# Two attention decode blocks on one core: heads in quads instead of pairs, 64 KB rows per transfer

## The chip, the core and the metric

The kernel runs on one core of a Trainium2 chip. The core has five engines with queues of their own: TensorE (PE, matrix products into PSUM; its weight loads are shown as PEld), VectorE (DVE), ScalarE (ACT), GpSimd (POOL) and SyncE (SP, which here only issues DMAs). Sixteen DMA engines move data between HBM and SBUF, the on-chip memory of 128 partitions. A semaphore is a counter that one queue raises and another waits for. The metric is the device time of one execution in microseconds (us), lower is better; the figure for the kernel before is the median of three runs.

## What is computed

Two blocks, A and B, of the same shape and with inputs of their own, whose outputs are put side by side. For each block:

```python
# x [1,1,512]  k_cache, v_cache [1,32,8192,128]  wq [512,4096]  wo [4096,512]   all bf16
q = (x @ wq).reshape(B, Sq, H, Dh).transpose(0, 2, 1, 3)       # 32 heads of 128
scores = jnp.einsum("bhqd,bhkd->bhqk", q, k_cache) * (Dh ** -0.5)
p = softmax(scores, axis=-1)
o = jnp.einsum("bhqk,bhkd->bhqd", p, v_cache)
y = o.transpose(0, 2, 1, 3).reshape(B, Sq, H * Dh) @ wo        # [1,1,512]
```

One query per head meets 8192 keys and values. Each element of the caches is used once. K and V of one head are 2 MB each; both blocks together hold 128 MB of K and 128 MB of V, and 16 MB of weights (MB here as 2^20 bytes).

## The kernel before

**Tiling.** Two heads, a pair, are worked on at a time: 32 pairs (`NP`), 16 of each block. Head 0 of a pair lies on partitions 0 to 63, head 1 on 64 to 127, and a partition holds T = 128 consecutive keys of 128 elements, which are 32 KB in one piece in HBM. So one transfer of K or V of a pair is 128 rows of 32 KB, 4 MB (`load_k`, `load_v`). K has two slots in SBUF (`kn`), V has two (`vn`), and a further buffer `wbuf` of 32 KB per partition holds the weights: first wq of A, later wo of A, then wo of B. wq of B is read into V's slot 1 before V needs it.

**What happens to a pair n.** DVE multiplies K in place by the query, which stands in `qbc` on each partition, in four pieces of 32 keys (`plan_mul`, L313). PE sums over the 128 elements of a key in groups: 16 matmuls with the identity as weights, 512 columns each, add into one PSUM bank for half the keys (`plan_red`, L322), and DVE sums the last 8 columns of each key (`plan_sr`, L331). Then the maximum (`plan_max` L337, `plan_gmax` L343 and L346: a transposing matmul and a reduction), its spreading over the partitions and the exponentials on ACT (`plan_exp`, L356 to L367), the sum of the exponentials and its reciprocal (`plan_sum`, L372 and L375). For the output PE runs 128 matmuls per pair (`plan_pv`, L388), each with 128 columns of V as weights and the two heads' probabilities as a moving operand of two columns, and DVE scales (`plan_o`, L398).

**Order.** The loop over n writes each engine's instructions out by hand, one pair deep: in round n, K of pair n is multiplied and reduced while the output of pair n-1 is made. On PE a round is `plan_sum(n-1)`, both halves of `plan_red(n)`, the first half of `plan_pv(n-1)`, `plan_gmax(n)`, the second half of `plan_pv(n-1)`, and the spreading of `plan_exp(n)`. PE's instructions for rounds 1 to 30 stand in a hardware loop of two rounds each (`_emit_loop`), whose waits count with registers; a register is raised after the instruction that waited (L113). Since two rounds stand in the body, each instruction names its slot of K and V outright. The other engines' programs are not looped.

**DMAs.** All large loads are issued by SP, in this order: wq of A, K 0, wq of B, K 1, V 0, and from then on K n+1 and V n in turn. K n+1 waits until `plan_red(n-1)` is done with its slot (`red_done`), V n until `plan_pv(n-2)` is (`pv_done`). The last V is cut into two halves, and wo of B follows in five parts that shrink (16, 8, 4, 2 and 2 heads; `WOG`), so that the output projection (`plan_wo`, L440) can follow them.

Of the kernel before, what the change touches and what calls it, by code (L numbers as in the profile page):

```python
# [74 lines left out]
def _emit_loop(e, rounds):  # L75
# [30 lines left out]
    with e.Fori(0, len(rounds)):  # L106
        for k, (waits, it) in enumerate(body):
            for i, (ctr, v, d) in enumerate(waits):
                e.wait_ge(ctr.sem, regs.get((k, i), v))
            _emit(e, [it])  # L110
            for i, (ctr, v, d) in enumerate(waits):
                if d:
                    e.reg_add(regs[k, i], regs[k, i], d)  # L113


def bass_concat_heads__mha_block_cached__gqa_block_cached__decode_kernel(
# [26 lines left out]
    HP = P // 2  # L143
    T = Sk // HP
    assert T == 128
    PA = H // 2
    NP = NA * PA
    NK = NV = 2
    CT = 32
    NCH = T // CT  # L150
    HT = T // 2
    DW = 512 // HT
# [3 lines left out]
    RG = [32, 16, 8, 4, 2]  # L156

    with ExitStack() as st:
# [7 lines left out]
        vn = sb("vn", [P, NV, T, Dh], BF16)  # L166
        wbuf = sb("wbuf", [P, C * H * Dh], BF16)
        wq_buf = [wbuf[:], vn[:, 1].rearrange("p t d -> p (t d)")]
        wq_sb = [b.rearrange("p (c n) -> p c n", c=C) for b in wq_buf]
        wo_sb = wbuf[:].rearrange("p (j n) -> p j n", n=NOUT)  # L170
        qbc = sb("qbc", [P, NP, Dh], BF16)
        pt = sb("pt", [P, 2, T, 2], BF16)
        s_sb = sb("s_sb", [P, 2, T], F32)
        xrow = sb("xrow", [1, NA, D], BF16)
        xb = sb("xb", [P, NA, C, P], BF16)
# [4 lines left out]
        hrow = sb("hrow", [1, 2, P], F32)  # L180
        m1 = sb("m1", [P, 2], F32)
        gm = sb("gm", [1, 2, 2], F32)
        negb = sb("negb", [P, NP], F32)
        rsum = sb("rsum", [P, 2, 2], F32)
        rinv = sb("rinv", [P, NP, 2], F32)
# [13 lines left out]
        acc = ps("acc", [P, 2, 512])  # L199
# [13 lines left out]
        s_wo = [ctr("s_wo%d" % i) for i in range(5)]  # L213
        s_v2 = ctr("s_v2")
        s_k = [ctr("s_k%d" % i) for i in range(NK)]
        s_v = [ctr("s_v%d" % i) for i in range(NV)]
# [20 lines left out]
        const(lambda e: e.memset(hrow[0:1, 0, 0:HP], 1.0), [i_h0])  # L237
        const(lambda e: e.memset(hrow[0:1, 1, HP:P], 1.0))
# [7 lines left out]

        def load_k(n):
            a, i = divmod(n, PA)
            src = ks[a][0, 2 * i:2 * i + 2].rearrange("h (p t) d -> (h p) (t d)", p=HP)
            k_in[n] = dma("SP", kn[:, n % NK].rearrange("p t d -> p (t d)"), src, s_k[n % NK],  # L250
                          [red_done.get(n - NK)])

        def load_v(n, parts=1):
            a, i = divmod(n, PA)
            src = vs[a][0, 2 * i:2 * i + 2].rearrange("h (p t) d -> (h p) (t d)", p=HP)
            dst = vn[:, n % NV].rearrange("p t d -> p (t d)")
            w = T * Dh // parts
            v_in[n] = [dma("SP", dst[:, i * w:(i + 1) * w], src[:, i * w:(i + 1) * w],
                           s_v2 if i else s_v[n % NV],
                           [q_done[1] if n == 1 else pv_done.get(n - NV)])  # L260
                       for i in range(parts)]
# [4 lines left out]
        def load_wo(a, g):  # L266
            h0, n = WOG[a][g]
            src = wos[a][h0 * Dh:(h0 + n) * Dh, :].rearrange("(p j) n -> p (j n)", p=P)
            wo_in[a, g] = dma("SP", wo_sb[:, h0:h0 + n, :].rearrange("p j n -> p (j n)"), src, s_wo[g],
                              [q_done[0] if a == 0 else wo_done[0]])  # L270
# [16 lines left out]
        def plan_q(a, j):  # L287

            def mm(e):
                r = None  # L290
                for hh in range(2):
                    for c in range(C):
                        w = wq_sb[a][:, c, 8 * j * Dh:8 * (j + 1) * Dh].rearrange(
                            "p (i h d) -> p i h d", h=2, d=Dh)[:, :, hh, :]
# [7 lines left out]
            n0 = a * PA + 4 * j  # L302
# [6 lines left out]
        mul_done, sr_done, p_done, m_done, r_done, o_done = {}, {}, {}, {}, {}, {}  # L309

# [6 lines left out]
        def plan_red(n, h):  # L317

            def mm(e):
                r = None  # L320
                for i in range(Dh // DW):
                    r = e.matmul(  # L322
                        rps[:, h, :].rearrange("p (t d) -> p t d", d=DW), ident[:],
                        kn[:, n % NK, h * HT:(h + 1) * HT, i * DW:(i + 1) * DW],
                        start=(i == 0), stop=(i == Dh // DW - 1))
                return r
            last = (h + 1) * HT // CT - 1
            red_done[n] = op("PE", mm, c_red, [i_ident, mul_done[n, last], sr_done.get((n - 1, h))])

        def plan_sr(n, h):  # L330
            sr_done[n, h] = op("DVE", lambda e: e.tensor_reduce(  # L331
                s_sb[:, n % 2, h * HT:(h + 1) * HT],
                rps[:, h, :].rearrange("p (t d) -> p t d", d=DW), AX.X, ALU.add),
                c_sr, [red_done[n], p_done.get(n - 2)])

        def plan_max(n):
            m_done[n] = op("DVE", lambda e: e.tensor_reduce(  # L337
                m1[:, n % 2:n % 2 + 1], s_sb[:, n % 2, :], AX.X, ALU.max), c_dve, [sr_done[n, 1]])
# [3 lines left out]
        def plan_gmax(n):  # L342
            m = op("PE", lambda e: e.matmul(mtp[0:1, 0:P], m1[:, n % 2:n % 2 + 1], ident_f[:],  # L343
# [3 lines left out]
                gm[:, n % 2, :], mtp[0:1, 0:P].rearrange("o (h p) -> o h p", h=2), AX.X, ALU.max),  # L347
                c_dve, [m])
# [3 lines left out]
        def plan_exp(n):  # L352
            def bc(e):
                r = None
                for h in range(2):
                    r = e.matmul(bmp[:, 0:1], hrow[0:1, h, :], gm[0:1, n % 2, h:h + 1],  # L356
                                 start=(h == 0), stop=(h == 1))
# [5 lines left out]
            wait("ACT", pv_done.get(n - 2))  # L363
            wait("ACT", i_pool)
            for h in range(2):
                q = slice(h * HP, (h + 1) * HP)
                p_done[n] = op("ACT", lambda e, h=h, q=q: e.activation(  # L367
                    pt[q, n % 2, :, h], s_sb[q, n % 2, :], AF.Exp, bias=negb[q, n:n + 1],
                    scale=scale, accum_out=rsum[q, n % 2, h:h + 1]), c_act)

        def plan_sum(n):
            m = op("PE", lambda e: e.matmul(misc[:, 0:2], ones_f[:], rsum[:, n % 2, :],  # L372
# [3 lines left out]
                rinv[:, n, :], misc[:, 0:2]), c_dve, [m])  # L376

        def plan_pv(n, t0, t1):
            parts = v_in[n]
            for i in range(t0 * len(parts) // T, (t1 * len(parts) - 1) // T + 1):  # L380
                wait("PE", parts[i])
            wait("PE", p_done[n])
            wait("PE", o_done.get(n - 2))

            def mm(e):
                r = None
                for t in range(t0, t1):
                    r = e.matmul(acc[:, n % 2, 0:2], vn[:, n % NV, t, :], pt[:, n % 2, t, :],  # L388
# [7 lines left out]
        def plan_o(n):  # L396
            a, i = divmod(n, PA)
            o_done[n] = op("DVE", lambda e: e.tensor_tensor(  # L398
                oD[:, a, 2 * i:2 * i + 2], acc[:, n % 2, 0:2], rinv[:, n, :], ALU.mult),
# [17 lines left out]
        def plan_relayout(a, g):  # L417
# [8 lines left out]
                c_dve, [sel_ready[n], o_done[a * PA + (h0 + n) // 2 - 1], z_free.get(z)])  # L426
# [5 lines left out]
        def plan_wo(a, g):  # L432
# [3 lines left out]
            def mm(e):  # L436
                r = None
                for j in range(h0, h0 + n):
                    for i in range(NQ):
                        r = e.matmul(qyp[:, i:i + 1], wo_sb[:, j, i * P:(i + 1) * P],  # L440
# [9 lines left out]
        def plan_out():  # L450
            m = op("PE", lambda e: e.matmul(bmp[0:NA * NQ, 0:P], yT[:].rearrange("p a q -> p (a q)"),  # L451
                                            ident[:], start=True, stop=True),
                   c_pe, [qy_free[0], nb_done[NP - 1]])
# [5 lines left out]
        L0, L1 = 1, 31  # L459
        marks = {}  # L460

        load_wq(0)
        load_k(0)
        load_wq(1)
        plan_sel()
        for j in range(4):
            plan_q(0, j)
        for n in range(NP + 1):
            marks[n] = len(pl.prog["PE"])
            last = n == NP  # L470
            if n == L1:
                plan_relayout(0, 0)
                for g in range(3):
                    plan_relayout(1, g)
                plan_wo(0, 0)
            if n + 1 < NP:
                load_k(n + 1)
            if n == 1:
                for j in range(4):
                    plan_q(1, j)  # L480
                marks[n] = len(pl.prog["PE"])
            if not last:
                load_v(n, 2 if n == NP - 1 else 1)
            if n == 12:
                load_wo(0, 0)
            if n == NP - 1:
                for g in range(len(WOG[1])):
                    load_wo(1, g)
            if not last:
                plan_mul(n, 0)  # L490
                plan_mul(n, 1)
            if n == L1:
                plan_y(0)
            if n > 0:
                plan_sum(n - 1)
            if not last:
                plan_red(n, 0)
                plan_mul(n, 2)
                plan_mul(n, 3)
                plan_sr(n, 0)  # L500
                plan_red(n, 1)
            if n > 0:
                plan_pv(n - 1, 0, HT)
            if not last:
                plan_sr(n, 1)
                plan_max(n)
                plan_gmax(n)
            if n > 0:
                plan_pv(n - 1, HT, T)
            if not last:  # L510
                plan_exp(n)
            if n > 0:
                plan_o(n - 1)
            if n >= L1:
                plan_relayout(1, n - L1 + 3)
        for g in range(len(WOG[1])):
# [4 lines left out]
        for name, at in (("SP", block.sync), ("PE", block.tensor), ("ACT", block.scalar),  # L521
                         ("DVE", block.vector), ("POOL", block.gpsimd)):
            @at
            def _(e, name=name):
                prog = pl.prog[name]
                if name != "PE":
                    _emit(e, prog)
                    return
                _emit(e, prog[:marks[L0]])
                _emit_loop(e, [prog[marks[n]:marks[n + 2]] for n in range(L0, L1, 2)])  # L530
# [29 lines left out]
```

## Time and profile before

| | |
|---|---|
| median of three runs (671.5 to 672.41) | 671.81 us |
| the profiled execution | 671.82 us, of which its span is 670.0 us |
| HBM read over the span | 285.21 MB (10^6 bytes), mean 426 GB/s |
| mean granted clock of TensorE | 0.742 |
| DVE's multiply of K, L313 | 128 times, 2283 ns each |
| DVE's waits for K of block B, L313 | 15, together 29.4 us |

The span runs from the first to the last instruction. Engines' busy times overlap each other; a busy share says only how full an engine is, not whether the end waits for it. The DMA rows of the page give the share of time in which the 16 DMA engines had a packet in hand. A packet is one row of a transfer: 32 KB for most here, less for parts of wo, and 4 bytes for the semaphore write with which each of the 16 engines ends its part of a transfer. The granted clock tells at what share of its full speed TensorE was allowed to run.

### The profile page before, as it was taken

The numbers are of one execution on the slowest core, as the hardware profiler recorded it, in microseconds if no ns is written. First come the engines' busy times: TensorE is split into PE (matmuls) and PEld (weight loads), VectorE is DVE, ScalarE is ACT, GpSimd is POOL, SyncE is SP. The second block draws the span as 40 slices with busy tenths as digits, with TensorE's granted clock in tenths as the row PEclk, the third lists the DMA queues.
The fourth block names the chain that finished last, engine by engine and source line by source line (L and its number), as shares of the span: only waits on it lengthen the run. The fifth ranks groups of instructions, "written<-read, shape, count | busy, mean of one in ns | idle before, by whom it ended". The sixth has DMA issues, their size and how long they took to land.

```text
span 670.0 us, 12431 instructions
## 1 busy us (share of the span) xinstructions
PE 473.1 (71%) x5711; PEld 276.2 (41%) x5711; DVE 359.6 (54%) x345; ACT 43.9 (7%) x171; POOL 2.1 (0%) x13
## 2 busy tenths in 40 slices
PE   2677876766777776664667776676687766768887
PEld 1224443434444343441344443344454334444456
DVE  1545456665555666515655556665555656555561
ACT  1120000000000000000000000000000000000000
POOL 1000000000000000000000000000000000000000
PEclk9977876667787666786677876667878766788766
DMA  9999999999999999999999999999999999999996
GB/s 376 438 433 422 427 436 435 432 428 425 439 434 434 426 425 436 438 430 430 423 436 438 430 430 425 436 436 432 430 425 436 436 431 428 428 434 434 433 416 272
DMA packets 10545, 285.39 MB, mean 426 GB/s; under 512 B 1186, under 2 KB 1188, under 8 KB 1572
## 3 DMA queue, kind: packets, MB, share of 16 engines
q1 hardware_dynamic: 10528, 285.22, 99.1%
q8 instruction: 8, 0.13, 0.1%
q14 instruction: 5, 0.04, 0.0%
q10 hardware_dynamic: 4, 0.00, 0.0%
HBM read 285.21 MB, written 0.00 MB: 426 GB/s over the span
## 4 chain that ended last, share of the span: by engine, by line
DMA 65%; PE 23%; DVE 7%; issue 4%; SPq 0%
DMA kn<-in_A_k_cache_dram 31%; DMA kn<-in_B_k_cache_dram 30%; PE rps L322 22%; DVE kn L313 7%; DMA wbuf<-in_B_wo_dram 3%; PE qyp L440 1%; PE acc L388 0%; SPq L222 0%; PE bmp L356 0%; PE misc L427 0%; DVE zb L423 0%; DVE o L429 0%; PE mtp L343 0%; PE bmp L451 0%; DVE out_q L454 0%
## 5 line engine op out<-in xcount | busy, mean ns | idle before, releaser
L322 PE MATMUL rps<-kn,ident 128*128 128x512 bf16 x1024 | 294.6, 459 | 134.6 <-DVE kn L313 134.6
L313 DVE TENSOR_TENSOR kn<-kn,qbc 128x4096 bf16<-128x4096 bf16 x128 | 286.8, 2283 | 88.4 <-DMA kn<-in_A_k_cache_dram 59.0
L322 PEld LDWEIGHTS rps<-kn,ident 128*128 128x128 bf16 x1024 | 114.6, 115 | 302.5 <-DVE kn L313 132.6
L388 PEld LDWEIGHTS acc<-pt,vn 128*128 128x128 bf16 x4096 | 110.5, 97 | 14.3 <-issue 6.9
L331 DVE TENSOR_REDUCE s_sb<-rps 128x64 f32<-128x512 f32 x64 | 44.3, 692 | 132.2 <-PE rps L322 132.2
L388 PE MATMUL acc<-pt,vn 128*128 128x2 bf16 x4096 | 112.8, 163 | 0.0
L372 PE MATMUL misc<-rsum,ones_f 128*128 128x2 f32 x64 | 18.2, 355 | 39.5 <-ACT pt L367 38.8
L360 ACT ACTIVATE negb<-bmp 128x1 f32<-128x1 f32 x32 | 5.5, 171 | 587.8 <-PE bmp L356 587.8
L372 PEld LDWEIGHTS misc<-rsum,ones_f 128*128 128x128 f32 x64 | 15.5, 301 | 42.9 <-ACT pt L367 41.3
L398 DVE TENSOR_TENSOR oD<-acc,rinv 128x2 bf16<-128x2 f32 x32 | 5.1, 160 | 47.6 <-PE acc L388 47.6
L367 ACT ACTIVATE pt<-s_sb,negb 64x128 bf16<-64x128 f32 x64 | 27.8, 435 | 1.9
L346 DVE TENSOR_REDUCE gm<-mtp 1x2 f32<-1x128 f32 x32 | 8.9, 279 | 27.8 <-PE mtp L343 27.8
L356 PE MATMUL bmp<-gm,hrow 1*128 1x1 f32 x128 | 23.2, 282 | 0.5 <-DVE gm L346 0.5
L356 PEld LDWEIGHTS bmp<-gm,hrow 1*128 1x128 f32 x128 | 20.6, 226 | 1.3 <-issue 0.7
L343 PE MATMUL mtp<-ident_f,m 128*1 128x128 f32 x64 | 12.1, 271 | 1.1 <-DVE m L337 1.1
L295 PE MATMUL qyp<-wbuf,xb 128*64 128x512 bf16 x32 | 7.7, 632 | 6.2 <-DMA wbuf<-in_A_wq_dram 4.1
L367 ACT ACTIVATION_READ_ACCUMULATOR pt<-s_sb,negb 64x1 f32 x64 | 11.6, 182 | 0.0
L337 DVE TENSOR_REDUCE m<-s_sb 128x1 f32<-128x128 f32 x32 | 9.2, 286 | 1.1
L295 PE MATMUL qyp<-vn,xb 128*64 128x512 bf16 x32 | 6.6, 554 | 2.3 <-ACT qbc L303 2.3
L440 PE MATMUL qyp<-o,wbuf 128*128 128x1 bf16 x256 | 7.6, 165 | 0.5 <-DMA wbuf<-in_B_wo_dram 0.3
L440 PEld LDWEIGHTS qyp<-o,wbuf 128*128 128x128 bf16 x256 | 7.2, 104 | 0.7 <-issue 0.4
L375 DVE RECIPROCAL rinv<-misc 128x2 f32<-128x2 f32 x32 | 5.3, 164 | 3.4 <-PE misc L372 3.4
(34 smaller groups left out, 27.4 us busy)
## 6 DMA issues: line engine op xcount, KB each, us to landing
kn<-in_A_k_cache_dram SPq DMA_DIRECT2D x16, 4096.0 KB, 25.3
vn<-in_A_v_cache_dram SPq DMA_DIRECT2D x16, 4096.0 KB, 31.4
kn<-in_B_k_cache_dram SPq DMA_DIRECT2D x16, 4096.0 KB, 25.4
vn<-in_B_v_cache_dram SPq DMA_DIRECT2D x15, 4096.0 KB, 31.5
wbuf<-in_A_wq_dram SPq DMA_DIRECT2D x1, 4096.0 KB, 12.4
vn<-in_B_wq_dram SPq DMA_DIRECT2D x1, 4096.0 KB, 30.8
wbuf<-in_A_wo_dram SPq DMA_DIRECT2D x1, 4096.0 KB, 41.2
vn<-in_B_v_cache_dram SPq DMA_DIRECT2D x2, 2048.0 KB, 18.5
```

The lines of the kernel that those rows point to most:

```text
L295: r = e.matmul(qyp[hh * HP:(hh + 1) * HP, :].rearrange("p (i d) -> p i d", d=Dh), xb[:, a, c, hh * HP:(hh + 1) * HP], w, start=(c == 0), s ...
L313: mul_done[n, c] = op("DVE", lambda e: e.tensor_tensor(k, k, qbc[:, n:n + 1, :].broadcast_to([P, CT, Dh]), ALU.mult), c_mul, [k_in[n], qbc ...
L322: r = e.matmul(rps[:, h, :].rearrange("p (t d) -> p t d", d=DW), ident[:], kn[:, n % NK, h * HT:(h + 1) * HT, i * DW:(i + 1) * DW], start= ...
L331: sr_done[n, h] = op("DVE", lambda e: e.tensor_reduce(s_sb[:, n % 2, h * HT:(h + 1) * HT], rps[:, h, :].rearrange("p (t d) -> p t d", d=DW ...
L337: m_done[n] = op("DVE", lambda e: e.tensor_reduce(m1[:, n % 2:n % 2 + 1], s_sb[:, n % 2, :], AX.X, ALU.max), c_dve, [sr_done[n, 1]])
L343: m = op("PE", lambda e: e.matmul(mtp[0:1, 0:P], m1[:, n % 2:n % 2 + 1], ident_f[:], start=True, stop=True), c_pe, [m_done[n], i_identf, g ...
L346: gm_done[n] = op("DVE", lambda e: e.tensor_reduce(gm[:, n % 2, :], mtp[0:1, 0:P].rearrange("o (h p) -> o h p", h=2), AX.X, ALU.max), c_dv ...
L356: r = e.matmul(bmp[:, 0:1], hrow[0:1, h, :], gm[0:1, n % 2, h:h + 1], start=(h == 0), stop=(h == 1))
L367: p_done[n] = op("ACT", lambda e, h=h, q=q: e.activation(pt[q, n % 2, :, h], s_sb[q, n % 2, :], AF.Exp, bias=negb[q, n:n + 1], scale=scale ...
L372: m = op("PE", lambda e: e.matmul(misc[:, 0:2], ones_f[:], rsum[:, n % 2, :], start=True, stop=True), c_pe, [p_done[n], misc_free[0]])
L388: r = e.matmul(acc[:, n % 2, 0:2], vn[:, n % NV, t, :], pt[:, n % 2, t, :], start=(t == 0), stop=(t == T - 1))
L440: r = e.matmul(qyp[:, i:i + 1], wo_sb[:, j, i * P:(i + 1) * P], o2[:, a, j:j + 1], start=(j == 0 and i == 0), stop=(j == H - 1 and i == NQ ...
```

## The change

Four heads, a quad, are worked on at a time: 16 rounds (`NM`) in place of 32. A head now lies on 32 partitions, and each partition holds T = 256 keys, 64 KB in one piece. One transfer of K or V is 128 rows of 64 KB, 8 MB. K has two slots of this size, V has one, and `wbuf` is gone: both blocks' wq are read into V's slot, both blocks' wo into the K slot of quad 14 after it has been reduced, and x and its spread copy `xb` lie in K's slot 1 at the start.

```diff
-    HP = P // 2
+    G = 4
+    HP = P // G
     T = Sk // HP
-    NK = NV = 2
-    CT = 32
+    NK = 2
+    CT = 64
+    VLAST = (0, T // 2, T // 2 + CT, T)
...
-        vn = sb("vn", [P, NV, T, Dh], BF16)
-        wbuf = sb("wbuf", [P, C * H * Dh], BF16)
-        wq_buf = [wbuf[:], vn[:, 1].rearrange("p t d -> p (t d)")]
+        vn = sb("vn", [P, T, Dh], BF16)
+        wq_buf = [flat(vn[:])[:, a * W:(a + 1) * W] for a in range(NA)]
+        KX, KW = 1, (NM - 2) % NK
+        wo_sb = [flat(kn[:, KW])[:, a * W:(a + 1) * W].rearrange("p (j n) -> p j n", n=NOUT)
+                 for a in range(NA)]
+        xb = flat(kn[:, KX])[:, 0:NA * C * P].rearrange("p (a c m) -> p a c m", a=NA, c=C)
...
         def load_k(n):
+            k_in[n] = dma("SP", flat(kn[:, n % NK]), quad(ks, n), s_k[n % NK],
+                          [q_done[1] if n == KX else red_done.get(n - NK)])
+        def load_v(n, cuts=(0, T)):
+            dst, src = flat(vn[:]), quad(vs, n)
+            v_in[n] = [(t0, dma("SP", dst[:, t0 * Dh:t1 * Dh], src[:, t0 * Dh:t1 * Dh], s_v[i],
+                                [q_done[1] if n == 0 else pv_done[n - 1]]))
+                       for i, (t0, t1) in enumerate(zip(cuts, cuts[1:]))]
         def load_wo(a, g):
...
+                              s_wo[a][g], [red_done[NM - 2]])
```

The probabilities, the scores, their sums and the output's PSUM bank (`pt`, `s_sb`, `rsum`, `acc`) have one buffer where they had two. DVE multiplies in four pieces of 64 keys, and PE and DVE reduce each piece by itself (16 matmuls and one `plan_sr` for each), where a pair had two. PE's loop has one round in its body, 15 times; K's slot comes from the loop's counter, so the matmuls of `plan_red` take their address from a register.

```diff
-    with e.Fori(0, len(rounds)):
+    with e.Fori(0, len(rounds)) as r:
+        enter(r)
...
+                    if slot[0] is None:
+                        k = kn[:, n % NK, t, d]
+                    else:
+                        k = kn[:, bass.ds(slot[0], 1), t, d].rearrange("p o t d -> p (o t) d")
...
+                def enter(r):
+                    slot[0] = (r + L0) % NK
```

The order of a round and of the ends is written anew:

```diff
+        load_wq(0)
+        load_wq(1)
+        load_k(0)
...
+        for n in range(NM):
+            if n + 1 < NM:
+                load_k(n + 1)
+            else:
+                load_wo(0, 0)
+                load_wo(1, 0)
+            plan_mul(n, 0)
+            if n > 0:
+                plan_sum(n - 1)
+            plan_red(n, 0)
+            plan_mul(n, 1)
+            plan_red(n, 1)
+            plan_sr(n, 0)
+            plan_mul(n, 2)
+            plan_red(n, 2)
+            plan_sr(n, 1)
+            plan_mul(n, 3)
+            plan_sr(n, 2)
+            if n > 0:
+                plan_pv(n - 1, 0, T)
+                plan_o(n - 1)
+            plan_red(n, 3)
+            plan_sr(n, 3)
+            plan_max(n)
+            plan_gmax(n)
+            plan_exp(n)
+            load_v(n, VLAST if n == NM - 1 else (0, T))
+        for g in range(1, len(WOG[1])):
+            load_wo(1, g)
+        plan_relayout(0, 0)
...
+        plan_wo(1, 0)
+        plan_sum(NM - 1)
+        for t0, t1 in zip(VLAST, VLAST[1:]):
+            plan_pv(NM - 1, t0, t1)
+        plan_o(NM - 1)
+        for g in range(1, 3):
+            plan_wo(1, g)
+        for g in range(3, len(WOG[1])):
+            plan_relayout(1, g)
+        for g in range(3, len(WOG[1])):
+            plan_wo(1, g)
```

So `plan_pv(n-1)`, 256 matmuls in one run, stands on PE ahead of the last quarter of `plan_red(n)`, and DVE's `plan_o(n-1)`, which waits for it, ahead of the last `plan_sr(n)`. V n is issued when `plan_pv(n-1)` is done, K n+2 when `plan_red(n)` is. The last V comes in three parts (4, 2 and 2 MB), behind wo of A and the first half of wo of B, and the four smaller parts of wo of B come last.

In PE's program as built, each of the 64 `plan_red` matmuls of a loop round has one instruction of fused register operations ahead of it (three operations; five for the first of a round) that works out its address. The loop's body has 730 PE instructions, weight loads counted, for one round of four heads; before it had 673 for two rounds of two heads.

## Prediction

> **What bounds the kernel now.** I read the slices of the span first, then the DMA queues, the chain that ended last, and one round of the timeline.
>
> ```profile
> DMA  9999999999999999999999999999999999999996
> DMA packets 10545, 285.39 MB, mean 426 GB/s; under 512 B 1186, under 2 KB 1188, under 8 KB 1572
> q1 hardware_dynamic: 10528, 285.22, 99.1%
> DMA 65%; PE 23%; DVE 7%; issue 4%; SPq 0%
> ```
>
> The DMA engines have a packet in hand in every slice, 99.1% of the span on the one queue. The chain names PE and DVE too, but only where it follows the release of K's slot; the queue never ran dry there. The packet records (start, duration, bytes of each) confirm it: the bulk runs from 1.85 to 666.6 us, and its packets add up to 663.5 us per engine, so all idling together is some 1.3 us. After the last packet come 3.4 us: its notice, 8 matmuls, the copy, the store. The kernel is a DMA stream with 1.85 us ahead of it and 3.4 behind.
>
> One round before (a pair), from the timeline:
>
> ```profile
> 403.51 4.49 DVE L313 TENSOR_TENSOR kn<-kn,qbc 128x4096 bf16<-128x4096 bf16 x2 [2.20 <-DMA kn<-in_B_k_cache_dram]
> 408.06 9.41 PE L322 MATMUL rps<-kn,ident 128*128 128x512 bf16 x32 [4.53 <-DVE kn L313]
> 417.31 1.75 PE L388 MATMUL acc<-pt,vn 128*128 128x2 bf16 x64
> 417.50 0.33 SPq L222 DMA_DIRECT2D kn<-in_B_k_cache_dram  x1
> 421.08 0.33 SPq L222 DMA_DIRECT2D vn<-in_B_v_cache_dram  x1
> 422.94 4.49 DVE L313 TENSOR_TENSOR kn<-kn,qbc 128x4096 bf16<-128x4096 bf16 x2 [1.68 <-DMA kn<-in_B_k_cache_dram]
> ```
>
> DVE starts a pair when K lands, every 19.5 us, and waits for it; K and V are released 15 us and 11 us before the queue reaches them. Compute is covered by DMA.
>
> **What the change saves in the stream.** The bytes stay the same; the packets get larger. Median packet durations by size: 2 KB 84 ns, 4 KB 159, 8 KB 311, 16 KB 614, 32 KB 1218. Twice the half minus the whole is 9, 7, 8 and 10 ns: a fixed price of some 9 ns per packet. No packet of 64 KB is in the trace; extended by the same step it takes 2 x 1218 - 9 = 2427 ns. The bounds for this unknown: the split keeps 32 KB pieces (saving nothing), or the fixed price is 10 ns. I take 9. Sixty-two full transfers (7936 rows of 32 KB) become 31 (3968 of 64 KB); the last V has 128 rows of 32 KB and 256 of 16 KB in both. So 3968 x 9 ns / 16 engines = 2.2 us. SP's loads fall from 73 to 42, each ends with 16 semaphore packets of 9 ns: 31 x 9 ns = 0.3 us. Together -2.5 us, between 0 and -2.8.
>
> The Trainium skill, "DMA: Bandwidth & Descriptors", section "Latency and other measured facts", speaks against wider rows: row pitches at large powers of two slow HBM copies, 214 GB/s falling to 207 at 512 KiB and 164 at 2 MiB. Here the 32 KB pitch shows nothing of it (1st and 99th percentile of the 32 KB packets 1213 and 1225 ns) and the new pitch is 64 KB, far below. By the rule's first step (3.3%) an estimate would be some 20 us more; by the row, nothing. I go by the row.
>
> **Whether compute stays covered.** A quad's K and V pass in 16 packets per engine, 16 x 2.427 = 38.8 us; V n-1 lands half a period after K n. With S the landing of K n, from these rows:
>
> ```profile
> 408.10:412.70 4.60, 4.60 (x11) 1.59 (x12) 0.50 0.94 406
> 413.00:417.00 4.00, 4.00 (x20) 1.85 (x19) 1.00 1.05 451
> L388 PE MATMUL acc<-pt,vn 128*128 128x2 bf16 x4096 | 112.8, 163 | 0.0
> L331 DVE TENSOR_REDUCE s_sb<-rps 128x64 f32<-128x512 f32 x64 | 44.3, 692 | 132.2 <-PE rps L322 132.2
> ```
>
> (The first two are L322's stretches of one round: matmuls in brackets, then the granted clock.) A red matmul takes 0.42 us at clock 0.50 and 0.21 at 1.00; the clock rises some 5 us after PE begins. One multiply of 64 keys is two of 2283 ns, 4.5 us.
>
> - DVE mul 0 to S+4.5. PE red 0, cold: 11 at 0.42, 5 at 0.21, to S+10.4. Red 1 to S+13.8. DVE sr 0 waits for red 0, so mul 2 ends at S+15.6; red 2 to S+19.1; mul 3 at S+20.8.
> - V n-1 has landed at S+19.4. PV is 256 matmuls; 64 took 1.75 us (also at clock 0.50 in the tail: 128 in 3.55), so 7.0 us to S+26.4. That releases V n.
> - Red 3, assumed cold again after PV, 6 us to S+32.4: K n+2 is released. Sr 0.7, maximum 0.4, transposing matmul and reduction 1.2: DVE is free at S+34.8.
>
> K n+1 lands at S+38.8, so a round has 4 us to spare. V n is released at S+26.4 and the queue reaches it at S+38.8: 12 us. K n+2, S+32.4 against S+58: 26 us. The single V slot costs nothing because K n+1 fills the queue meanwhile; without that cover the queue would idle the 7 us of PV each round, 112 us in all. ACT's four exponentials (0.435 us for 128 columns, at most twice that for 256, plus 0.18 each) take up to 4.2 us after DVE's end, before the next multiply has ended. SP's waits are in the order of release (V n, then K n+2), so neither holds up the other.
>
> **Register addresses.** Each red matmul has a fused register operation ahead. Rows: 37 ns for a fused one, 32 for a single (L113). If it ran beside the array: 0; in series: 64 x 37 ns = 2.4 us per round, inside the 4 to spare. How PE issues a matmul whose address is in a register is not in the trace; bounds are 0.21 us (hidden) and the nearest instruction whose addresses a queue works out, SP's DMA issue, 0.33 + 0.04 = 0.37 us. I take hidden, as the register rows are nearest. At 0.37 red 1 and 2 grow by 5.1 us: 39.9 against 38.8, 1.1 x 15 rounds plus some 7 at the start: +23.
>
> **Start.** Wq of both land at about 12.5 and 22.8 us (in the trace K 0, second 4 MB in line, was there at 22.86). Two groups of 16 matmuls for block B (8 took 1.93 us, plus 0.75 until the next) end near 31; K 1 and V 0 are issued then, while K 0 transfers until 1.85 + 2 x 9.75 + 19.4 = 40.8. DVE's first multiply moves from 22.9 to 41.2 with no gap in the stream. Round 0 without PV ends at 41.2 + 26.7 = 67.9, later than K 1 landed; PV 0 ends at 67.9 + 26.2 = 94.1 and releases V 1, which the queue reaches at 99.0. This is the thinnest place: 5 us, of which about 1 goes from issue to first packet.
>
> **End.** Wo of A and half of B (14.6 us of packets) lie between V 14 and the last V, whose wait for PV 14 (S+26.4) ends before S+34. After its last part 5.1 us of wo follow. PV's 64 matmuls, the scaling, 32 and 16 matmuls of L440 fit beside these; two relayouts of 0.65 us remain, so the last matmuls come some 0.2 us later than before. Its 3.4 us become 3.6.
>
> **Sum.** 671.82 - 2.2 - 0.3 + 0.2 = 669.5 us; the profiled execution lies 0.01 us over the median. Own range 668.8 to 670.4.
>
> **Rivals.**
> - Slower: PE's rounds outgrow the transfers. If a red matmul took 0.42 us throughout (the clock held at 0.50, or the register path that slow), the chain is 4.5 + 64 x 0.42 + 7.0 + 2.9 = 41.3 us, 2.5 over; with V 1's gap of 9 and V 15's of 7, 14 x 2.5 + 16 = 51: 720 us. It decides from about 0.38 us per matmul. For: PV drops the clock, and red 3 comes after it. Against: in each round before, the clock rose within 6 us of red's start. With the milder 0.37 it gives 692. Chance 0.15 for both.
>
> The skill's "TensorE: Matmul & The Clock Gate", Part 1, says full clock comes after some 3.4 us of sustained activity and is lost after an idle window. The trace's 4.8 us is later; by the page's figure red 0 would end 1.4 us sooner, which the wait for K hides.
>
> - No change: rows are cut to 32 KB pieces, or 64 KB packets have no lower price: 671.82 - 0.3 + 0.2 = 671.7. For: no such packet is shown. Against: the price has been fixed over four doublings. Chance 0.13.
> - Start gap alone: reds in round 0 and 1 at 0.42 rather than my mix delay V 1 by up to 9 us past its margin: 670 to 679, middle 674. Against: nothing loads PE's clock there differently. Chance 0.09.
> - Packets of 64 KB a little slower per byte: 1% of 622 us is 6.2, so 676. For: no such row. Against: 32 KB rows spread over 1% only, 1213 to 1225 ns. Chance 0.04.
>
> **Numbers.** Forecast 0.59. Range 668.5 to 679: it holds all but the first rival, 0.85, less 0.03 at the edges. Faster than 670.5 (0.2%, about what a measurement here can tell from none): 0.59 less the upper edge plus little, 0.58. Within: 0.16, from no change and the edges. Slower: 0.26.
>
> **What would show it.** Right: 64 KB packets of about 2427 ns, the DMA row full in all slices, DVE waiting some 4 us per round for K, SP waiting only for PE with the queue still filled. Wrong: holes in the DMA row (at 95 us: start; in each round: PE), red matmuls over 0.38 us on average, packets of 32 KB, or packets over 2450 ns.

## The result, and the profile after

| | before | after |
|---|---|---|
| median, 5 runs each | 671.81 us (671.5 to 672.41) | 719.92 us (719.38 to 720.44) |
| ratio, 95% interval | | 1.0716 (1.0701 to 1.073) |
| profiled execution: span | 670.0 us | 718.7 us |
| first to last large packet | 1.85 to 666.6 us | 1.84 to 711.9 us |
| large packets' time per engine | 663.5 us | 670.1 us |
| stretches in which under 8 of the 16 DMA engines were busy (over 0.3 us each) | none | 15, together 38.5 us |
| after the last packet | 3.4 us | 6.8 us |

The last four rows are summed from the packet records. The span grew by 48.7 us: 38.5 of holes in the stream, 6.6 of packet time, 3.4 of tail; the rest is at the packets' edges. The 6.6 are a net figure: the larger packets save 2.7 us, and in 14 of the 15 holes the first packet of each engine behind the hole takes some 3.1 us instead of 2.42. The page of the changed kernel shows the same: the slices, the queue and the chain that ended last.

```profile
PEclk9558786676667577677668677667757667766865
DMA  9999948999999998999999898989899898989785
q1 hardware_dynamic: 6064, 285.22, 93.3%
PE 69%; DVE 16%; ACT 8%; DMA 6%; issue 2%; SPq 0%
```

The DMA row, all nines but the last digit before, has a dent in the sixth slice, then an 8 now and then, and in the second half in nearly every other slice. The chain was 65% DMA before; now it is PE, DVE and ACT, and DMA only until the first K has landed. The kernel is no longer a stream of transfers but a chain of computation. One stretch of the stages table (busy us and count of PE, PEld, DVE, ACT, POOL, then clock, DMA share, GB/s) shows the dent, the hole near 100 us:

```profile
99.50:112.00 12.50, 12.50 (x275) 8.77 (x274) 5.79 (x4) 0.00 (x0) 0.00 (x0) 0.77 0.08 25
```

And one round, from the timeline, with lines left out (start, duration, what; in brackets the idle time ahead of it and what ended it). Below, mul, red and sr with a number stand for `plan_mul`, `plan_red` and `plan_sr` of that piece of a quad:

```profile
308.88 6.65 PE L401 MATMUL acc<-pt,vn 128*128 128x4 bf16 x256
315.39 6.45 PE L334 MATMUL rps<-kn,ident 128*128 x16
315.56 0.33 SPq L230 DMA_DIRECT2D vn<-in_A_v_cache_dram  x1
321.88 0.33 SPq L230 DMA_DIRECT2D kn<-in_B_k_cache_dram  x1
323.71 4.40 DVE L320 TENSOR_TENSOR kn<-kn,qbc 128x8192 bf16<-128x8192 bf16 x1
328.86 0.59 PE L385 MATMUL misc<-rsum,ones_f 128*128 128x4 f32 x2 [3.82 <-ACT pt L380]
329.31 9.78 PE L334 MATMUL rps<-kn,ident 128*128 x32
329.49 0.18 DVE L388 RECIPROCAL rinv<-misc 128x4 f32<-128x4 f32 x1 [1.38 <-PE misc L385]
329.59 4.39 DVE L320 TENSOR_TENSOR kn<-kn,qbc 128x8192 bf16<-128x8192 bf16 x1
339.13 0.69 DVE L343 TENSOR_REDUCE s_sb<-rps 128x64 f32<-128x512 f32 x1 [5.14 <-PE rps L334]
339.74 4.42 DVE L320 TENSOR_TENSOR kn<-kn,qbc 128x8192 bf16<-128x8192 bf16 x1
344.29 5.67 PE L334 MATMUL rps<-kn,ident 128*128 x16 [5.20 <-DVE kn L320]
```

Red 0 and red 1 run as one block of 32 matmuls from 329.3 to 339.1. DVE's reduction of piece 0 (L343) starts when the whole block is over, not after its first 16. Multiply 2 stands behind that reduction on DVE, so red 2 cannot start before 344.3, and PE idles 5.2 us. In that time the granted clock falls to half (at 341.65) and red 2 takes 5.67 us, where the same 16 matmuls take 3.6 at full clock. From one red 0 to the next is 41.0 us in the later rounds; the transfers need 38.8.

The reason lies in two lines of the changed kernel. Every piece writes the same entry of the dictionary, and the round records red 1 ahead of the reduction of piece 0:

```python
red_done[n] = op("PE", mm, c_red, [...])          # plan_red(n, c), for every c
... c_sr, [red_done[n], p_done.get(n - 1)])       # plan_sr(n, c): the newest red recorded, not its own
```

`plan_sr(n, 0)` therefore waits for red 1 and `plan_sr(n, 1)` for red 2. The kernel before recorded `plan_sr(n, 0)` ahead of the second `plan_red`, so the same entry was the right one there. In a round with PV, sr 1's wait lies beside PV, on which red 3 has to wait anyway; round 0 has no PV, and there red 2 and red 3 both start late and at half clock. Its maximum comes at 78.0 us, against 66.3 us in the first run below, in which this wait alone is mended; that delay, passed on to V 1, is the hole near 100 us. The waits of DVE add up to (total us, times, longest):

```profile
DVE s_sb L343 <- PE rps L334: 272.5, 48, 6.2
DVE rinv L388 <- PE misc L385: 23.1, 16, 2.5
```

### The profile page after: what moved, and what is told of

It reads as the page before. It is cut to its first block, busy times and chain, and to the rows that moved or that the text cites. A ratio compares the mean times of both kernels' runs of the same rounds, so it can differ in the third digit from the quotient of the medians.

```text
span 718.7 us, 12990 instructions
## 1 busy us (share of the span) xinstructions
PE 500.1 (70%) x5647; PEld 269.8 (38%) x5647; DVE 341.7 (48%) x217; ACT 62.5 (9%) x151; POOL 2.8 (0%) x15
## 4 chain that ended last, share of the span: by engine, by line
PE 69%; DVE 16%; ACT 8%; DMA 6%; issue 2%; SPq 0%
PE rps L334 48%; PE acc L401 15%; DVE kn L320 11%; ACT pt L380 7%; DMA kn<-in_A_k_cache_dram 6%; DVE s_sb L343 3%; PE bmp L368 3%; PE misc L385 1%; PE qyp L453 1%; DVE m L349 1%; PE mtp L355 1%; DVE gm L358 1%; ACT negb L372 0%; PE misc L440 0%; DVE zb L436 0%
## 5 line engine op out<-in xcount | busy, mean ns | idle before, releaser
L334 PE MATMUL rps<-kn,ident 128*128 (+1 forms) x1024 | 348.4, 519 | 107.6 <-DVE kn L320 107.6
L320 DVE TENSOR_TENSOR kn<-kn,qbc 128x8192 bf16<-128x8192 bf16 x64 | 282.0, 4408 | 38.2 <-DMA kn<-in_A_k_cache_dram 38.2
L334 PEld LDWEIGHTS rps<-kn,ident 128*128 128x128 bf16 x1024 | 128.5, 128 | 314.8 <-issue 262.3
L343 DVE TENSOR_REDUCE s_sb<-rps 128x64 f32<-128x512 f32 x64 | 44.2, 690 | 272.5 <-PE rps L334 272.5
L401 PE MATMUL acc<-pt,vn 128*128 128x4 bf16 x4096 | 107.0, 165 | 4.2 <-issue 4.2
L380 ACT ACTIVATE pt<-s_sb,negb 32x256 bf16<-32x256 f32 x64 | 54.9, 858 | 2.1 <-ACT negb L372 0.2
L385 PE MATMUL misc<-rsum,ones_f 128*128 128x4 f32 x32 | 9.4, 364 | 57.5 <-ACT pt L380 57.5
L385 PEld LDWEIGHTS misc<-rsum,ones_f 128*128 128x128 f32 x32 | 8.0, 311 | 58.8 <-ACT pt L380 58.8
L380 ACT ACTIVATION_READ_ACCUMULATOR pt<-s_sb,negb 32x1 f32 x64 | 15.9, 248 | 0.0
L301 PE MATMUL qyp<-vn,kn 128*32 128x512 bf16 x64 | 7.7, 623 | 10.9 <-DMA vn<-in_B_wq_dram 5.1
L453 PE MATMUL qyp<-o,kn 128*128 128x1 bf16 x256 | 7.7, 165 | 0.8 <-issue 0.5
L301 PEld LDWEIGHTS qyp<-vn,kn 128*32 128x32 bf16 x64 | 2.3, 128 | 15.6 <-issue 6.4
```

The source lines that it names most:

```text
L301: r = e.matmul(qyp[hh * HP:(hh + 1) * HP, :].rearrange("p (i d) -> p i d", d=Dh), xb[:, a, c, hh * HP:(hh + 1) * HP], w, start=(c == 0), s ...
L320: mul_done[n, c] = op("DVE", lambda e: e.tensor_tensor(k, k, qbc[:, n:n + 1, :].broadcast_to([P, CT, Dh]), ALU.mult), c_mul, [k_in[n], qbc ...
L334: r = e.matmul(rps[:, c % 2, :].rearrange("p (t d) -> p t d", d=DW), ident[:], k, start=(i == 0), stop=(i == Dh // DW - 1))
L343: sr_done[n, c] = op("DVE", lambda e: e.tensor_reduce(s_sb[:, c * CT:(c + 1) * CT], rps[:, c % 2, :].rearrange("p (t d) -> p t d", d=DW), ...
L380: p_done[n] = op("ACT", lambda e, h=h, q=q: e.activation(pt[q, :, h], s_sb[q, :], AF.Exp, bias=negb[q, n:n + 1], scale=scale, accum_out=rs ...
L385: m = op("PE", lambda e: e.matmul(misc[:, 0:G], ones_f[:], rsum[:], start=True, stop=True), c_pe, [p_done[n], misc_free[0]])
```

## The experiments

The ratios are to runs of the kernel before, made beside each kernel on the same chip. A round is called covered when DVE waits in it for K's transfer.

**Own waits.** Each reduction waits for its own piece.

```diff
-            red_done[n] = op("PE", mm, c_red, [
+            red_done[n] = red_part[n, c] = op("PE", mm, c_red, [
...
-                c_sr, [red_done[n], p_done.get(n - 1)])
+                c_sr, [red_part[n, c], p_done.get(n - 1)])
```

> Each DVE reduction (plan_sr) of a piece waits for its own piece's matmuls instead of the newest planned ones; nothing else changes. Theory (the shared wait): sr 0 starts some 3.5 us sooner in a round, mul 2 and red 2 with it, red 2 falls from 5.7 to about 3.4 us because PE no longer idles 5 us ahead of it; the round falls from 40.95 us to the 38.8 of the transfers, the 1.5 us hole of each round and the 12.7 us hole near 100 us close: 668 to 674 us. Rival (register addresses slow the matmuls): under 1% change, 713 to 720. Rival (PE at half clock after PV is what costs): only the wait shrinks, 700 to 710.

Measured: 671.33 us (12 runs, 670.36 to 673.32), ratio 0.9999 (0.9987 to 1.001). A round from its timeline, with lines left out (the first line is the block of red 0 and red 1, cut by the window of the view):

```profile
379.51 9.29 PE L335 MATMUL rps<-kn,ident 128*128 x31
385.38 0.69 DVE L344 TENSOR_REDUCE s_sb<-rps 128x64 f32<-128x512 f32 x1 [2.07 <-PE rps L335]
385.99 4.42 DVE L321 TENSOR_TENSOR kn<-kn,qbc 128x8192 bf16<-128x8192 bf16 x1
390.55 3.62 PE L335 MATMUL rps<-kn,ident 128*128 x16 [1.75 <-DVE kn L321]
394.01 6.74 PE L402 MATMUL acc<-pt,vn 128*128 128x4 bf16 x256
400.60 5.73 PE L335 MATMUL rps<-kn,ident 128*128 x16
413.19 4.42 DVE L321 TENSOR_TENSOR kn<-kn,qbc 128x8192 bf16<-128x8192 bf16 x1 [4.92 <-DMA kn<-in_B_k_cache_dram]
```

The reduction now starts in the middle of the block, red 2 follows red 1 after 1.75 us at full clock, and the next round's multiply waits 4.9 us for K: the transfers set the pace again, 38.7 us from round to round. The holes are gone but for 1.4 us near 100 us. So mending this one wait takes back the whole loss of 48 us; that it does not cause that loss by itself is shown by the third run below.

**No register addresses.** Two rounds in the loop's body, 14 of the 15 looped, slots named outright.

```diff
-        L0, L1 = 1, NM
+        L0, L1 = 1, NM - 1
...
-                    slot[0] = (r + L0) % NK
+                    slot[0] = None
...
-                _emit_loop(e, [prog[marks[n]:marks[n + 1]] for n in range(L0, L1)], enter)
+                _emit_loop(e, [prog[marks[n]:marks[n + 2]] for n in range(L0, L1, 2)], enter)
```

> The loop body holds two rounds (14 of the 15), K's slot is named outright, no register addresses; everything else as in the changed kernel. Theory (the shared wait): same time within 0.5%, 716 to 723. Rival (register addresses): the rounds fall below 39 us, under 690.

Measured: 723.49 us, ratio 1.0764 (1.0748 to 1.0779), 0.5 us above the theory's range. Rounds stay at 41.0 us. In the changed kernel the register operations are there, 46 ns each, but hidden: red 1 takes 3.62 us with them and without:

```profile
L334 PEldq FUSED_REGOPS  x960: 46/46/122, 84.3 to 685.6; - x192
```

The register addresses cost nothing that can be seen. The 3.6 us more fall into the first pass of the longer body: a hole of 5.9 us at 152 us instead of 1.1, with a stop of PE of 4.37 us in the middle of PV 1 that no semaphore ended.

**Sum of the exponentials later.** `plan_sum(n-1)` behind red 0 and mul 1; the shared wait stays.

```diff
-            if n > 0:
-                plan_sum(n - 1)
             plan_red(n, 0)
             plan_mul(n, 1)
+            if n > 0:
+                plan_sum(n - 1)
             plan_red(n, 1)
```

> plan_sum of the previous quad stands behind red 0 on PE and behind mul 1 on DVE; the shared wait stays. Theory: the exponentials leave the chain at a round's start, 1.2 to 1.5 us per round, 15 rounds: 700 to 708 us; the transfers' 38.8 us per round are not reached. Rival (the exponentials are the whole excess over the transfers): below 690.

Measured: 685.53 us, ratio 1.0201 (1.0186 to 1.0215), better than the theory's 700 and inside its rival's range. In the round shown above PE takes up red 0 only at 329.31, after ACT's four exponentials and the sum, though multiply 0 ended at 328.1, and multiply 1 waits behind the reciprocal. With that gone the rounds last 39.7, 37.8, 37.6 and 38.5 us in turn, 38.4 on average: just under the 38.8 of the transfers. That is 2.6 us less where 1.2 to 1.5 were taken out of the chain; the reductions lose less time to half clock (red 0 takes 5.4 us on average instead of 6.3). What is left of the loss is the hole near 100 us (11.6 us) and the tail (6.5 us after the last packet). So in the later rounds the shared wait alone does not put a round over the transfers; it takes both, and removing either is enough. The hole near 100 us, which comes from round 0, stays nearly whole here.

**Both edits.**

> Both edits together: own wait for each reduction, and plan_sum behind red 0. Theory: the rounds are bound by the transfers already with the first edit, so no more than 2 us below it: 667 to 673 us. Rival (a second wait still holds the rounds in the first edit): 5 us or more below it.

Measured: 670.79 us (11 runs), ratio 0.9988 (0.9978 to 0.9999). As the theory had it: nothing more to gain in the rounds, which last 38.7 us in both. Its packets take 660.75 us per engine, 3.65 us follow the last.

**A warm PE.** The changed kernel with 20 matmuls of the identity ahead of red 2 into a spare bank; their result is not used.

```diff
             plan_mul(n, 2)
+            plan_warm()
             plan_red(n, 2)
```

> The changed kernel with its shared wait, and 20 more matmuls of the identity into a spare PSUM bank ahead of red 2 in each round, in the time in which PE waits for mul 2; their result is not used. Theory (the wait costs twice, as a hole of 5.2 us and as half clock after it): red 2 falls from 5.6 to 3.5 us, the round from 41.0 to 38.9 or less, 676 to 692 us. Rival (the clock has no part): 716 to 723.

Measured: 681.0 us, ratio 1.0136 (1.012 to 1.0151).

```profile
396.74 4.48 PE L347 MATMUL dmy<-ident 128*128 128x512 bf16 x20
396.94 0.69 DVE L353 TENSOR_REDUCE s_sb<-rps 128x64 f32<-128x512 f32 x1 [5.44 <-PE rps L335]
402.11 3.62 PE L335 MATMUL rps<-kn,ident 128*128 x16 [0.89 <-DVE kn L321]
```

The reduction still waits for the whole block, but red 2 takes 3.62 us instead of 5.67. Rounds fall to 37.6 us, and to the transfers' 38.7 once the chain has caught up with them; no hole is left but the one near 100 us. More work on PE makes the kernel 39 us faster. Of the 3.4 us that a round loses, 2.05 are red 2's half clock; red 3 and red 0 give the rest (5.56 us instead of 6.48, 5.95 instead of 6.35). So without the half clock the wait does not put the round over the transfers either.

**PV in the hole.** The changed kernel with `plan_pv(n-1)` ahead of red 2.

> The changed kernel with its shared wait; PV of the previous quad moved ahead of red 2, into the hole. Theory: sr 1 waits for red 2 as sr 0 does for red 1, which PV had hidden; the hole of some 5 us moves ahead of red 3 with its half clock, the round stays within 1 us: 705 to 722 us. Rival (PV's place after red 2 is the fault): the hole is filled, rounds under 38.8, below 690.

Measured: 692.87 us, ratio 1.0326 (1.0308 to 1.0343): between the two ranges. The hole did move ahead of red 3, as the theory said:

```profile
386.90 5.75 PE L334 MATMUL rps<-kn,ident 128*128 x16 [5.20 <-DVE kn L320]
...
409.29 6.83 PE L401 MATMUL acc<-pt,vn 128*128 128x4 bf16 x256
415.97 4.87 PE L334 MATMUL rps<-kn,ident 128*128 x16
```

(The first line is red 3 of one round, the others are PV and the next red 2 in the round behind it.) But rounds fell to 39.3 us (40.15 and 38.36 in turn), not within 1 us of 41.0, so the size was misjudged. Red 2 is no shorter on average (4.9 and 6.4 us in turn), but red 3 takes 5.4 us instead of 6.5 and red 0 5.8 instead of 6.3. The holes of the rounds shrink to 1.3 us at most; one of 5.0 us at 648 us and the 11.3 us after the last packet make up much of what is left.

**Rows of 32 KB.** Both edits, each transfer of K and V cut into two.

> Both edits (own waits, plan_sum behind red 0), and each K and V transfer cut into two of 32 KB rows; same bytes and order. Theory (a packet has a fixed price of some 8 ns, 64 KB rows save it once per 64 KB): the packets' time grows by 2.2 to 2.7 us per engine to 663.3, the run by as much, 672.5 to 674.5. Rival (64 KB rows save nothing): 670.3 to 671.5.

Measured: 672.05 us (11 runs), ratio 1.0009 (1.0 to 1.0018), 1.26 us over the kernel with both edits, which ran on another chip (by the ratios 0.2%, 1.4 us). Packets take 663.73 us per engine against 660.75: 64 KB rows save 3.0 us of the stream. The run shows less, because here the hole near 100 us is 0.25 us instead of 1.7. The expected time was missed by 0.5 us; the saving itself is there.

**PV 0 earlier.** Both edits, round 1 out of the loop with PV 0 ahead of red 1, relayouts ahead of wo's parts 1 and 2.

> Both edits of the run before (own waits, plan_sum behind red 0), and round 1 taken out of the loop with PV 0 ahead of its red 1, and the last two relayouts ahead of wo's parts 1 and 2. Theory: V 1 is released some 8 us sooner, so the 1.4 to 1.7 us hole near 100 us closes, in the runs in which it was longer too; the last matmuls come 0.3 us sooner: 668.5 to 669.5 us, 0.3 to 0.5% under the kernel before. Rival (the hole comes from the late start of round 0, not from PV 0's place): 670.5 to 671.

Measured: 670.26 us (11 runs), ratio 0.9978 (0.9969 to 0.9988), above the theory's range and just under its rival's. The hole near 100 us is closed and another of 1.1 us stands at 138 us: the loop's body is now entered in round 2, and there PE stops in the middle of PV 1 with no semaphore to wait for:

```profile
127.26 4.41 PE L402 MATMUL acc<-pt,vn 128*128 128x4 bf16 x167
135.73 2.53 PE L402 MATMUL acc<-pt,vn 128*128 128x4 bf16 x89 [4.06 <-issue]
```

The packet records show what it waits for: a packet of 16 KB on the queue that the page calls "instruction" runs from 133.21 to 134.28 us, and PE goes on 1.5 us later. With both edits alone such packets start at 89.73 and 97.21 us, and PE resumes PV 0 at 92.04 and 99.61 after stops of 2.0 and 4.0 us. So the stops go with fetches of code.

**K 0 in two halves.** With both edits and the tail's order as above (first), and in the changed kernel alone (second).

```diff
+            if n == 0:
+                for i, sem in enumerate((s_kh, s_k[0])):
+                    w = slice(i * T * Dh // 2, (i + 1) * T * Dh // 2)
+                    k_in[0, i] = dma("SP", flat(kn[:, 0])[:, w], quad(ks, 0)[:, w], sem)
+                return
...
-                c_mul, [k_in[n], qbc_ready[n]])
+                c_mul, [k_in[0, 2 * c // NCH] if n == 0 else k_in[n], qbc_ready[n]])
```

> Own waits and plan_sum behind red 0, as before; the first transfer of K in two halves of 32 KB rows with a semaphore each, so that round 0's first two multiplies start with the first half; and the last two relayouts ahead of wo's parts 1 and 2. Theory (the hole near 100 us comes from the late start of round 0, which waits for 8 MB behind both wq): round 0 starts near 31.5 us instead of 41.6, V 1 is released some 9 us before the queue reaches it, the hole closes: 668.3 to 669.6 us, 0.3 to 0.5% under the kernel before. Rival (fetching the loop's code holds PE in round 1 and opens a hole all the same): 670 or more.

> The changed kernel with its shared wait and its order; only the first transfer of K comes in two halves. Theory (from round 1 on the chain of rounds of 41 us sets the end, not the transfers): the whole chain moves forward by the 9 to 10 us that round 0 starts sooner, 708 to 713 us; rounds stay at 41.0. Rival (the transfers set the end and the hole is theirs alone): 718 to 721.

Measured, first: 668.21 us (668.11 to 668.52), ratio 0.9949 (0.9935 to 0.9962): 0.5% under the kernel before. The two stops for code in PV 0 are still there (2.0 and 3.7 us), but V 1 is released early enough all the same. No hole is left, and the page's DMA rows are those of a stream again:

```profile
DMA  9999999999999999999999999999999999999997
q1 hardware_dynamic: 6208, 285.22, 99.2%
```

Second: 711.73 us, ratio 1.0592 (1.0576 to 1.0609). The chain of 41 us rounds starts earlier (the first maximum at 66.8 instead of 78.0 us), ends as much earlier, less a longer first round, and is otherwise unchanged: from round 1 on the rounds set the end of the changed kernel, not the transfers.

## Why the prediction was wrong

- **What bounds the kernel before** held: with the rounds covered, four variants (own waits, both edits, rows of 32 KB, PV 0 earlier) come out within 0.3% of it, and the packets' time sets them. One reading is off, on the safe side: a load of V took 31.5 us from issue to landing, 9.75 of them in transfer, so V was released some 22 us before the queue reached it, not 11.
- **The saving in the stream** (-2.5 us, 64 KB packets of 2427 ns) held: packets of 64 KB have a median of 2418 ns after and 2420 in the kernel with own waits; the stream shrank by 2.7 us (663.5 to 660.8), 3.0 against equal order with 32 KB rows. The Trainium skill, "DMA: Bandwidth & Descriptors", section "Latency and other measured facts", has slower copies at row pitches of 512 KiB and more; at the 64 KB of this case nothing of it shows.
- **The step that failed**: "DVE sr 0 waits for red 0, so mul 2 ends at S+15.6; red 2 to S+19.1." The edit was costed by the order of the calls, without following which mark the wait carries. In its place the runs showed: sr 0 waits for red 1, which holds multiply 2 some 3.5 us longer, empties PE for 5.2 us and sends red 2 out at half clock, 5.7 us instead of 3.6. With the wait mended, the forecast's round holds: PV ends 26.3 us after K has landed (S+26.4 forecast) and DVE waits 4.9 us for K (4 forecast).
- **A second step failed beside it**: the exponentials were to end "before the next multiply has ended". Their time was near (3.5 us, at most 4.2 forecast), but the cycle was closed over DVE (maximum to next multiply) and not over ACT and the sum on PE, which stand ahead of red 0 and, through the reciprocal, ahead of multiply 1. That is 1.2 to 1.5 us per round (2.6 came off when it was taken out); alone it is hidden, together with the first it is not.
- **The rival "PE's rounds outgrow the transfers"** gave 720 us, and 719.92 was measured. That the numbers meet is luck, since the cause is partly wrong: it needed red matmuls of 0.42 us throughout or over 0.38 on average, by the clock or by register addresses. Measured, a red matmul took 0.34 us on average (6.28, 3.62, 5.66 and 6.39 us for the four pieces), under its threshold, and what made the round long was the wait. Half clock was part of it, register addresses were not. Its holes (9 us at the start, 2.5 per round, 7 at the end) came out as 12.7, 1.5 and 6.4, and the 9.3 us by which its packets take longer than those of the kernel with both edits (670.1 against 660.75) stood in none of the terms.
- **Start**: the margin of 5 us for V 1 was not there even with own waits; V 1 was issued at 99.9 us, not at 94.1, and a hole of 1.4 us remained. PE stops there for 1.7 and 3.7 us in PV 0, while its loop's code comes in for the first time. Code loading was in no term. A side estimate is off too, that red 0 could end 1.4 us sooner: 1.4 us less at half clock saves half of that, 0.7 us.
- **End**: 3.6 us after the last packet was right for the covered kernels (3.65). In the changed kernel it is 6.8, since PE reaches PV 15 when all its parts have landed, and its code again comes late (packets of 16 KB on the instruction queue at 701.13 and 707.38 us):

```profile
701.64 0.38 PE L401 MATMUL acc<-pt,vn 128*128 128x4 bf16 x9
703.55 3.55 PE L401 MATMUL acc<-pt,vn 128*128 128x4 bf16 x128 [1.53 <-issue]
709.75 3.31 PE L401 MATMUL acc<-pt,vn 128*128 128x4 bf16 x119 [2.65 <-issue]
```

Open: why the times of the kernel with own waits spread over 3 us, as do those of the kernel before, is not seen in one profile of each. Whether the size of the packets in flight lengthens the stops for code stays open too: with rows of 32 KB the two stops in PV 0 were 2.3 and 2.6 us, against 2.0 and 4.0 with 64 KB, one profile each.

## What to carry to other kernels

When a schedule is written by hand over marks kept in a dictionary, follow each wait to the mark that it really gets after the reordering; a key without the piece's number waits for the newest piece recorded. Close a round's cycle over every engine in turn, not only over the one that seems to pace it, and compare the longest with the transfers' round. And a transfer that doubles in size also doubles what the first computation waits for: cutting just the first one gave 2.6 us (670.79 to 668.21; of it 0.25 us lie behind the last packet, where the tail's order was changed too).

## What the hardware showed unexpectedly

- The granted clock changes only on a grid of 3.413 us, and the rounds of a chain that sets its own pace fall on it. The changed kernel's rounds are 40.96 us, which is 12 steps, in the register and the static version alike; with the warm PE they are 37.55 us, 11 steps, until the transfers take over; with PV in the hole two rounds take 78.51 us, 23 steps; with the sum moved, four rounds of 39.7, 37.8, 37.6 and 38.5 us repeat, 153.6 together, 45 steps. Rounds that the transfers set are 38.7 us, no whole number of steps. The Trainium skill, "TensorE: Matmul & The Clock Gate", "Part 1: The HAM clock gate", gives a free-running window of this length; the locking of a kernel's period to it is what the runs add; why the rounds settle there was not tried by itself. A microsecond in a chain can so cost more or less than itself: 1.2 to 1.5 us taken out gave 2.6 with the sum moved.
- 256 matmuls of four columns, at 26 ns each and without a gap, do not hold the clock. In the round of the kernel with own waits it falls at 398.08 us, in the middle of PV. Red 3 behind PV took 4.9 to 6.4 us in the covered rounds, but 3.63 in round 0, where no PV stands ahead of it; with PV 0 ahead of red 1, red 1 of that round took 5.93 us and red 3 3.63.
- After a hole the packets themselves are slower: 64 KB packets had a mean of 2461 ns and a 95th percentile of 2921 in the changed kernel, against 2424 and 2427 with own waits. It is the first packet of each engine: 222 of the 238 that took over 2.5 us start at the end of a hole, 15 or 16 at each of 14 holes. So each hole of 1.5 us costs some 0.7 us more, and the two make up the 2.2 us by which a round outlasts the transfers.
- Stops of 0.5 to 4.4 us come where code is run for the first time; where PV has two, they are 128 matmuls apart, 256 PE instructions with the weight loads. The Trainium skill, "Runtime: NRT & Kernel Launch", "Instruction fetch mechanics", names blocks of 256 instructions and calls crossing one mostly hidden; at 26 ns per matmul it was not.
